# P times V in two PSUM banks of 256 queries, instead of one bank of 512, in a gated mix of segment attention and SwiGLU

## The chip, the cores and the metric

The kernel runs on one NeuronCore of a Trainium2 chip. The metric is the device time of one execution in microseconds (us), taken as the median of three timed executions; beside it there is one profiled execution, whose trace all readings come from. The engines are called by what they do here: TensorE multiplies matrices and writes its sums to PSUM, VectorE and ScalarE read PSUM and write SBUF, GpSimd works on SBUF alone, and SyncE issues transfers.

## The reference

The input x has 2048 rows of 640. The output is `g * a + (1 - g) * b`, with a gate `g = sigmoid(x . gate_w)` per row, an attention branch a and a SwiGLU branch b with an inner width of 1728. The attention has 32 heads of 20 columns and walks over 4 segments of 512 rows. The part that matters here, for each head and segment:

```
logits = einsum("bhqd,bhkd->bhqk", qs, ks) * scale + mask      # causal within the segment
p      = softmax(logits)
a_dot  = einsum("bhqk,bhkd->bhqd", p, vs)
o      = g * a_mem + (1 - g) * a_dot        # a_mem: read from a running memory M, z
M, z   = M + phi(ks)^T vs,  z + sum(phi(ks))
```

## The kernel before

TensorE's order is written out by hand: the program order of matmuls is the order in which the Python code issues them. The other engines' orders come from a scheduler. All projections (`q`, `k`, `v`, `g` and `u` of the SwiGLU, `f` its down projection, `op` the output projection) are long runs of 128x128x512 matmuls, and they fill the time between short attention bursts, called visits here.

A quad is four heads. Each quad of attention has a large visit and a small one. In its large visit TensorE issues, without a projection between them, `s_fill` 0 and `t_fill` 0 and 1, then `pv_quad` of a quad from an earlier visit, then `t_fill` 3, `s_fill` 2, `t_fill` 2 and `s_fill` 1 (the list `VISITS`, line 758). `s_fill` (line 594) makes logits with queries on the partitions, and VectorE takes row maxima of them (line 609). `t_fill` (line 625) makes logits with keys on the partitions, and ScalarE takes their exponent out of PSUM into the tile P (line 641). `pv_quad` (line 650) multiplies the exponents by V: the four heads stand in four column groups of 32 of the array and run side by side. Key block kb needs only queries from 128 kb on, so the four key blocks give widths of 512, 384, 256 and 128 queries. An fp32 matmul appears in the trace as two instructions, so one quad has 32 of them. Its sums are one tile `o` of 128 x 512, which VectorE copies to the SBUF tile `oq` (line 659); a transfer stores `oq` to DRAM (line 661).

PSUM has 8 banks, and every tile in it takes one whole bank. `bank_tile` (line 111) gives the banks out in a queue:

```
k = free.pop(0)
ps = pp.tile([P, L], F32, tag=f"b{k}", name=name, bufs=1)
if hold:
    held[k] = -hold
else:
    free.append(k)
```

A projection's bank is held out of the queue until its last matmul (`filled`, line 122). At a large visit none is held, so a tile takes the bank of the tile that was taken eight places before it, and its first matmul waits until the last reader of that older tile has ended. An `s_fill` and a `t_fill` take two banks each, a `pv_quad` one. The first eight tiles of a visit are two of `s`, four of `t`, the `o`, and the first `t` of `t_fill` 3.

The readers of the projections' tiles that stand just ahead of a visit also run on VectorE or ScalarE: line 515 multiplies a `g` tile by the tanh that ScalarE made of it, line 521 reads a `u` tile, line 285 and then line 287 read a `q` or `k` tile (phi), and lines 536, 561, 563 and 816 read `f` and `op` tiles.

Of the kernel before, what the change touches and what calls it, by code (L numbers as in the profile page):

```python
# [17 lines left out]
P = 128  # L18
# [16 lines left out]
PSEG = ((0, 512), (512, 384), (1024, 256), (896, 128))  # L35
# [3 lines left out]
def gated_mix(ctx: ExitStack, tc: tile.TileContext, xT, wqk, wv, w13, w2, w2h, wo, beta, out):  # L39
    nc = tc.nc  # L40
# [70 lines left out]
    def bank_tile(name, hold=None):  # L111
# [8 lines that stand above are left out]
        return ps  # L120
# [447 lines left out]
    oall, heads, pairs = {}, {}, {}  # L568
# [80 lines left out]

    def pv_quad(p):  # L650

        ps = bank_tile(f"o{p}")
        for kb, (o, n) in enumerate(PSEG):
            for i in range(4):
                nc.tensor.matmul(ps[32 * i:32 * i + 32, kb * P:], heads[2 * p + i]["v"][:, kb],  # L655
                                 pairs[p + i // 2]["P"][:, i % 2, o:o + n],
                                 start=kb == 0, stop=kb == 3, skip_group_check=True)
        ot = sp.tile([P, L], F32, tag="oq", name=f"oq{p}", bufs=1)
        nc.vector.tensor_copy(ot, ps)
        c, h = heads[2 * p]["c"], heads[2 * p]["h"]  # L660
        nc.sync.dma_start(od[c][h:h + 4].rearrange("h e n -> (h e) n"), ot)
        q = p // 2 % 8
        for b in OUT.get(q, ()):
            after(8, o_load, c, b)
        if q == 7:
            after(6 if c < NSEG - 1 else 2, o_sums, c)
# [77 lines left out]
    def after(n, f, *a):  # L744
        soon.append([n, f, a])
# [15 lines left out]
    def attention():  # L761

        for m in range(-1, NQUAD + 2):
            for n in range(40):
                if m == -1 and n < 40 - LEAD:
                    continue

                todo = VISITS.get(n, ()) if m != 1 else {BIG: VISITS[BIG][:3], BIG + 6: VISITS[BIG][4:]}.get(n, VISITS.get(n, ()))
                todo = [(kind, m - q, f) for kind, q, *f in todo if 0 <= m - q < NQUAD]
                if todo:  # L770
                    yield "amid" if len(todo) < 4 else "between"
                    for kind, q, f in todo:
                        if kind == "o":
                            pv_quad(2 * q)
                        else:
                            (s_fill if kind == "s" else t_fill)(q, *f)
                    if n == SMALL and 0 <= m < NQUAD:
                        after(4, max_rows, 2 * m)
                elif n in ((24, 36) if m < 0 else (BIG + 7, SMALL + 1)) and m + 1 < NQUAD:
                    load_pair(2 * (m + 1) + (n > BIG + 7 if m >= 0 else n > 24))  # L780
                tick()
                yield m
# [262 lines left out]
```

## Time and profile before

| | us |
|---|---|
| median of three timed executions | 1108.73 (1108.67 to 1112.61) |
| the profiled execution | 1108.07 |
| its span, first to last instruction | 1106.4 |
| TensorE matmuls busy | 1095.1 |
| VectorE busy | 593.5 |
| GpSimd busy | 583.3 |
| ScalarE busy | 381.2 |

The profiled execution is 0.66 us below the median, and 1.67 us of it lie outside the span. The granted clock of TensorE is 1.000 over the span. Busy times of TensorE are modelled from pipelined instructions; where it matters, the starts of its instructions are read instead, in the timeline. In the timeline's rows the first column is the start of an instruction or of a merged run, the second its duration, both in us, and square brackets hold the idle time of the engine ahead of it with what ended it. Buffer numbers are left out of tile names.

### The profile page before, as it was taken

How to read it: one execution, taken by the hardware profiler on the slowest of the kernel's cores; microseconds unless marked ns; L12 is line 12 of the kernel's file. 1: busy time of each engine (PE TensorE's matmuls, PEld its weight loads, DVE VectorE, ACT ScalarE, POOL GpSimd, SP SyncE). 2: the span in 40 equal slices, each digit the busy share in tenths (PEclk: the TensorE clock that was granted, in tenths of full speed). 3: DMA queues.
4: the chain of work that ended last, by engine and by line, in shares of the span. 5: the costliest groups of instructions: out<-in, count | busy, mean ns of one | idle time of the engine just before them, and what ended most of it. 6: DMA issues, size and time to landing. Idle time of an engine off the chain costs nothing.

```text
span 1106.4 us, 17867 instructions
## 1 busy us (share of the span) xinstructions
PE 1095.1 (99%) x6285; PEld 854.0 (77%) x6285; DVE 593.5 (54%) x1708; ACT 381.2 (34%) x826; POOL 583.3 (53%) x729
## 2 busy tenths in 40 slices
PE   9999999999999999999999999999999999999997
PEld 7988877777777777787977777777777777777786
DVE  5032564355555554366154678875557665551645
ACT  6244233343233122145244543424333332233120
POOL 5055556366366363565175547556764555565253
PEclk9999999999999999999999999999999999999999
DMA  8266943335165132535268967455654443432122
GB/s 314 102 212 220 281 117 82 95 82 127 47 164 125 57 78 94 156 98 191 96 202 271 287 204 193 103 157 138 166 139 111 103 104 90 117 105 86 52 79 95
DMA packets 87545, 153.20 MB, mean 138 GB/s; under 512 B 11584, under 2 KB 25184, under 8 KB 87456
## 3 DMA queue, kind: packets, MB, share of 16 engines
q1 hardware_dynamic: 63040, 106.30, 30.5%
q0 software_dynamic: 20384, 38.68, 15.6%
q10 hardware_dynamic: 4032, 7.08, 1.8%
q8 instruction: 50, 0.82, 0.3%
q14 instruction: 39, 0.32, 0.1%
HBM read 96.56 MB, written 54.54 MB: 137 GB/s over the span
## 4 chain that ended last, share of the span: by engine, by line
PE 94%; DVE 3%; ACT 1%; DMA 1%; issue 1%; ACTq 0%; SPq 0%; DVEq 0%
PE g L253 17%; PE u L253 16%; PE f L555 16%; PE k L253 6%; PE v L381 6%; PE op L805 6%; PE o L655 6%; PE q L253 5%; PE s L602 5%; PE t L635 4%; PE nd L348 1%; PE pm L445 1%; PE q L323 1%; DVE junk L609 1%; PE pkt L430 1%
## 5 line engine op out<-in xcount | busy, mean ns | idle before, releaser
L609 DVE CUSTOM_DVE_ANT_0 junk<-s,mask 128x256 bf16<-128x256 f32 (+3 forms) x512 | 250.3, 489 | 105.9 <-PE s L602 73.6
L641 ACT ACTIVATE P<-t 128x512 f32<-128x512 f32 (+1 forms) x384 | 172.4, 538 | 190.5 <-PE t L635 153.3
L253 PE MATMUL g<-X,W 128*128 128x512 f32 x840 | 208.7, 398 | 0.0
L175 POOL TENSOR_TENSOR W<-wr,W 128x640 fp32r<-128x640 f32 (+1 forms) x126 | 200.2, 1595 | 2.3
L174 POOL CAST W<-wr 128x640 fp32r<-128x640 f32 (+1 forms) x126 | 90.9, 726 | 208.9 <-PE f L555 47.0
L253 PE MATMUL u<-X,W 128*128 128x512 f32 x780 | 196.8, 399 | 0.0
L555 PE MATMUL f<-ht,W 128*128 128x512 f32 x820 | 196.6, 397 | 0.0
L645 POOL TENSOR_SCALAR_AFFINE_SELECT P<-P 128x256 f32<-128x256 f32 x192 | 94.0, 498 | 181.1 <-ACT P L641 180.7
L253 PEld LDWEIGHTS g<-X,W 128*128 128x128 f32 x840 | 156.0, 188 | 36.5 <-issue 0.4
L555 PEld LDWEIGHTS f<-ht,W 128*128 128x128 f32 x820 | 152.8, 188 | 36.5 <-DVE acc L536 0.4
L253 PEld LDWEIGHTS u<-X,W 128*128 128x128 f32 x780 | 144.1, 188 | 34.4 <-ACT P L641 0.3
L107 POOL TENSOR_TENSOR ht<-ft,ht 128x512 fp32r<-128x512 f32 x52 | 67.0, 1289 | 91.9 <-ACT ht L106 91.3
L579 POOL DMA_DIRECT2D qk<-qkd x128 | 83.3, 652 | 0.3
L602 PE MATMUL s<-qk 60*128 60x256 f32 (+3 forms) x512 | 78.2, 346 | 1.3 <-DVE fu L515 1.0
L253 PE MATMUL k<-X,W 128*128 128x512 f32 x300 | 77.0, 404 | 0.0
L655 PE MATMUL o<-P,vg 128*32 128x512 f32 (+3 forms) x1024 | 75.5, 436 | 1.4 <-DVE on L735 1.4
L514 ACT ACTIVATE ft<-g 128x512 f32<-128x512 f32 x52 | 31.1, 599 | 125.8 <-PE g L253 114.8
L381 PE MATMUL v<-W,X 128*128 128x320 f32 (+1 forms) x480 | 71.9, 311 | 0.4 <-ACT P L641 0.4
L515 DVE SCALAR_TENSOR_TENSOR fu<-ft,g 128x512 f32<-128x512 f32 x52 | 35.6, 685 | 68.3 <-ACT ft L514 59.2
L381 PEld LDWEIGHTS v<-W,X 128*128 128x128 f32 x480 | 71.0, 189 | 1.1 <-ACT P L641 0.6
L106 ACT CAST ht<-ft 128x512 fp32r<-128x512 f32 x52 | 32.2, 619 | 112.0 <-DVE ft L521 111.9
L563 DVE TENSOR_TENSOR acc<-f,acc 128x512 f32<-128x512 f32 x65 | 44.7, 689 | 44.8 <-PE f L555 44.6
(120 smaller groups left out, 1200.6 us busy)
## 6 DMA issues: line engine op xcount, KB each, us to landing
qk<-qkd POOLq DMA_DIRECT2D x128, 240.0 KB, 4.2
wr<-in_w_dram SPq DMA_DIRECT2D x80, 320.0 KB
qkd<-qs SPq DMA_DIRECT2D x20, 512.0 KB
qkd<-ks SPq DMA_DIRECT2D x20, 512.0 KB
od<-oq SPq DMA_DIRECT2D x32, 256.0 KB
wr<-in_wo_dram SPq DMA_DIRECT2D x20, 320.0 KB
vg<-vd SPq DMA_DIRECT2D x16, 336.0 KB
xr<-in_xT_dram SPq DMA_DIRECT2D x20, 256.0 KB
```

The lines of the kernel that those rows point to most:

```text
L107: (lo or nc.gpsimd.tensor_sub)(dst[:, 1], src, dst[:, 0].bitcast(F32))
L174: nc.gpsimd.tensor_copy(w[:, 0, :n], raw[:, :n])
L175: nc.gpsimd.tensor_sub(w[:, 1, :n], raw[:, :n], w[:, 0, :n].bitcast(F32))
L253: nc.tensor.matmul(ps, w[:, a, kb * P:(kb + 1) * P], x[:, b, kb, :], start=n == 0, stop=n == 14)
L381: nc.tensor.matmul(ps[:, :n1 - n0], x[:, a, kb, lb * P:(lb + 1) * P], wvt[kb][:, b, n0:n1], start=n == 0, stop=n == 14)
L555: nc.tensor.matmul(ps, w, h, start=n == 0, stop=n == len(ms) - 1)
L579: here(nc.gpsimd.dma_start(t[64 * i:64 * i + RH], qkd[c][RH * (h + i):RH * (h + i + 1)]))
L602: nc.tensor.matmul(ps[i][:, o:o + w], q[:, qb * P:(qb + 1) * P], key[:, :w], start=n == 0, stop=n == len(todo) - 1, skip_group_check=True)
L609: nc.vector.tensor_tensor_reduce(out=junk[:, :w], in0=ps[i][:, o:o + w], in1=mask[:, L - w:], scale=1.0, scalar=-3.0e38, op0=ALU.add, op1= ...
L641: last["exp"] = nc.scalar.activation(pairs[2 * m + k]["P"][:, i, o:o + n], ps[i][:, b:b + n], AF.Exp, scale=SCALE)
L645: nc.gpsimd.affine_select(d, d, pattern=[[0, 2], [0, n], [1, P]], base=0, channel_multiplier=-1, compare_op=ALU.is_ge, fill=0.0)
L655: nc.tensor.matmul(ps[32 * i:32 * i + 32, kb * P:], heads[2 * p + i]["v"][:, kb], pairs[p + i // 2]["P"][:, i % 2, o:o + n], start=kb == 0 ...
```

## The change

`pv_quad` takes two banks instead of one. The first holds queries 0 to 255 and gets key blocks 0 (256 wide) and 1 (128 wide). The second holds queries 256 to 511 and gets key blocks 0, 1 and 2 (256 wide each) and 3 (128 wide). The products are the same; the 16 matmuls of a quad become 24 (32 and 48 instructions). VectorE's copy of 512 columns becomes two of 256 columns; the first waits for the first bank only. The order of all other matmuls stays as it was, but every tile after the first half of `o` takes its bank one place further along the queue.

```diff
     def pv_quad(p):
 
-        ps = bank_tile(f"o{p}")
-        for kb, (o, n) in enumerate(PSEG):
-            for i in range(4):
-                nc.tensor.matmul(ps[32 * i:32 * i + 32, kb * P:], heads[2 * p + i]["v"][:, kb],
-                                 pairs[p + i // 2]["P"][:, i % 2, o:o + n],
-                                 start=kb == 0, stop=kb == 3, skip_group_check=True)
+        halves = [bank_tile(f"o{p}_{x}")[:, :256] for x in range(2)]
+        for x, ps in enumerate(halves):
+            todo = [(kb, max(P * kb, 256 * x), 256 * x + 256) for kb in range(2 * x + 2)]
+            for n, (kb, q0, q1) in enumerate(todo):
+                o = PSEG[kb][0] + q0 - P * kb
+                for i in range(4):
+                    nc.tensor.matmul(ps[32 * i:32 * i + 32, q0 - 256 * x:], heads[2 * p + i]["v"][:, kb],
+                                     pairs[p + i // 2]["P"][:, i % 2, o:o + q1 - q0],
+                                     start=n == 0, stop=n == len(todo) - 1, skip_group_check=True)
         ot = sp.tile([P, L], F32, tag="oq", name=f"oq{p}", bufs=1)
-        nc.vector.tensor_copy(ot, ps)
+        for x, ps in enumerate(halves):
+            nc.vector.tensor_copy(ot[:, 256 * x:256 * x + 256], ps)
         c, h = heads[2 * p]["c"], heads[2 * p]["h"]
         nc.sync.dma_start(od[c][h:h + 4].rearrange("h e n -> (h e) n"), ot)
```

## The prediction

> **What bounds the kernel now.** I read the page first: busy times, then the chain that ended last.
>
> ```profile
> span 1106.4 us, 17867 instructions
> PE 1095.1 (99%) x6285; PEld 854.0 (77%) x6285; DVE 593.5 (54%) x1708; ACT 381.2 (34%) x826; POOL 583.3 (53%) x729
> ...
> PE 94%; DVE 3%; ACT 1%; DMA 1%; issue 1%; ACTq 0%; SPq 0%; DVEq 0%
> ```
>
> TensorE (PE) carries 94% of the chain, and nothing else more than 3%. So the end moves by what TensorE's stream gains or loses; a faster VectorE (DVE) pays only where TensorE waits for it. I therefore looked at one large visit in the timeline, the first that has an `o`, starting at 172.24.
>
> ```profile
> 172.24 2.36 PE L655 MATMUL o<-P,vg 128*32 128x512 f32 x32
> 172.48 0.68 DVE L515 SCALAR_TENSOR_TENSOR fu<-ft,g 128x512 f32<-128x512 f32 x1
> 172.69 0.13 PEld L655 LDWEIGHTS o<-P,vg 128*32 128x32 f32 x4 [0.30 <-issue]
> 173.08 0.68 DVE L609 CUSTOM_DVE_ANT_0 junk<-s,mask 128x512 bf16<-128x512 f32 x1
> 173.12 0.13 PEld L655 LDWEIGHTS o<-P,vg 128*32 128x32 f32 x4 [0.30 <-issue]
> 173.44 0.13 PEld L655 LDWEIGHTS o<-P,vg 128*32 128x32 f32 x4 [0.19 <-issue]
> 173.77 0.56 PEld L655 LDWEIGHTS o<-P,vg 128*32 128x32 f32 x12 [0.19 <-issue]
> 174.53 0.50 PE L635 MATMUL t<-qk 62*128 62x512 f32 x2
> 174.66 0.69 DVE L659 COPY oq<-o 128x512 f32<-128x512 f32 x1 [0.89 <-PE o L655]
> 175.12 2.19 ACT L641 ACTIVATE P<-t 128x512 f32<-128x512 f32 x6 [0.96 <-PE t L635]
> 175.34 0.57 PE L602 MATMUL s<-qk 60*128 60x384 f32 x4
> 175.84 3.74 PE L253 MATMUL u<-X,W 128*128 128x512 f32 x15
> ```
>
> Two things are to be seen. First, the last `s_fill` of the visit waits for the copy: its second tile is the eighth after `o`, so it takes `o`'s bank, and the copy ends at 174.66 + 0.69 = 175.35, just after that fill began at 175.34. Second, the copy idles 0.89 us for TensorE before it can start. Where the copy is out of the way, the same fill is shorter:
>
> ```profile
> 557.78 2.36 PE L655 MATMUL o<-P,vg 128*32 128x512 f32 x32
> 559.65 0.69 DVE L287 SCALAR_TENSOR_TENSOR pk<-k,phi_t 128x512 f32<-128x512 f32 x1
> 560.40 0.50 PE L635 MATMUL t<-qk 62*128 62x512 f32 x2 [0.27 <-DVE pk L287]
> 561.22 0.40 PE L602 MATMUL s<-qk 60*128 60x384 f32 x4
> ```
>
> It takes 0.40 us here against 0.57: the wait is worth at most 0.17 us. This visit also shows the other kind of wait. The `t` tile after `o` takes the bank of the last projection tile ahead of the visit, a `k` here; line 287 ends with it at 559.65 + 0.69 = 560.34, and `t` starts 0.06 later, at 560.40. It is 2.62 us behind the start of `o`, against 2.29 (174.53 less 172.24) in the first visit. So 0.06 us is the price from a reader's end to TensorE's start.
>
> **Part 1: narrower matmuls.** A group is four instructions side by side, one per head; a quad has 8 groups before and 12 after, over the same columns. The weight loads start as each group begins: 172.69 to 173.12 is a 512-wide group, 0.43; 173.12 to 173.44 and 173.44 to 173.77 are 384-wide, 0.32 and 0.33. That is 0.108 per 128 columns in both, so nothing is left for a group as such; the rounding leaves at most 0.01. Four more groups in 32 quads are 128, so 0 to 1.3 us; a group cheaper than its columns is excluded by the same rows. I take 0.3, near the lower end, since 4 to 3 fits the two sorts of rows. The first group shows 0.45 (172.24 to 172.69), 0.02 over: the load of the first weights, which is exposed only after a pause.
>
> The Trainium skill speaks against such a split: "TensorEngine Tiling (Array Packing)", section Instruction Overhead, gives each matmul an overhead of about 60 cycles. By it, 16 more instructions in 32 quads at 25 ns (an estimate from that page and the 2.4 GHz of "TensorE: Matmul & The Clock Gate") would be 12.8 us, and the sum further down 18.5 instead of 6.0. The 0.43 and 0.32 above do not agree with it.
>
> **Part 2: the wait for the copy goes.** What the copies cost, by the nearest shapes:
>
> ```profile
> L609 DVE CUSTOM_DVE_ANT_0 junk<-s,mask 128x512 bf16<-128x512 f32 x128 | 88.2, 689 | 50.2 <-PE s L602 42.7
> L609 DVE CUSTOM_DVE_ANT_0 junk<-s,mask 128x256 bf16<-128x256 f32 x128 | 54.3, 424 | 38.1 <-PE s L602 30.9
> L641 ACT ACTIVATE P<-t 128x512 f32<-128x512 f32 x256 | 137.0, 600 | 190.5 <-PE t L635 153.3 <-DVE acc L563 18.7 <-DVE acc L816 9.0
> ```
>
> A row-maximum over 512 columns takes 689 ns, as the copy does (0.69), and one over 256 takes 424; so I give each half copy 0.42. The first starts when VectorE has done the maxima ahead of it, 173.08 + 0.68 = 173.76, and ends at 174.18. The second starts where the whole copy did, 174.66, and ends at 175.08, 0.27 earlier. After the change the last `s_fill` has the banks of the two halves, and both copies are over before 175.34. Its wait goes.
>
> What is late next is ScalarE. The projection that follows (175.84) takes the bank of the first `t` after `o`, whose exponent starts at 175.12 and lasts 0.60 by the group's mean: 175.72, plus 0.06 is 175.78. So 0.06 of the 0.17 is gained. Of the 32 visits with an `o` the last two have no such fill, and the three of part 3 that wait for line 287 or so start what follows behind ScalarE as well; 27 times 0.06 is 1.6. I take 1.5, since some fillers go straight on to the bank of the second `t` tile, which ScalarE frees later. Ends: 0, and 27 times 0.17 = 4.6 if ScalarE does not bind.
>
> **Part 3: a new wait at the second half.** The second half of `o` is now the eighth tile after the last projection tile ahead of the visit, a place that the `t` after `o` had before. That `t` came 2.29 us after `o`'s start; the second half is wanted after two groups of 256 and two of 128 columns, 6 times 0.108 = 0.65 us. The reader of that projection tile has 1.64 us less. Who is late is read visit by visit: the start of `o`, and the end of the reader.
>
> ```profile
> 342.09 2.36 PE L655 MATMUL o<-P,vg 128*32 128x512 f32 x32
> 341.29 0.69 DVE L521 SCALAR_TENSOR_TENSOR ft<-fu,u 128x512 f32<-128x512 f32 x1 [2.02 <-PE u L253]
> 976.35 2.36 PE L655 MATMUL o<-P,vg 128*32 128x512 f32 x32
> 976.60 0.68 DVE L515 SCALAR_TENSOR_TENSOR fu<-ft,g 128x512 f32<-128x512 f32 x1
> 512.43 2.36 PE L655 MATMUL o<-P,vg 128*32 128x512 f32 x32
> 513.68 0.68 DVE L287 SCALAR_TENSOR_TENSOR pq<-q,phi_t 128x512 f32<-128x512 f32 x1
> 629.55 2.36 PE L655 MATMUL o<-P,vg 128*32 128x512 f32 x32
> 631.36 0.69 DVE L287 SCALAR_TENSOR_TENSOR pq<-q,phi_t 128x512 f32<-128x512 f32 x1
> 632.11 0.50 PE L635 MATMUL t<-qk 62*128 62x512 f32 x2 [0.20 <-DVE pq L287]
> ```
>
> - A `u` tile (line 521) is read by 341.98, before `o` starts: no wait. Other kinds of tiles are no later than the 0.65.
> - A `g` tile is read by line 515 in the visit itself, since ScalarE's tanh comes between. It is the last projection in eight visits: the first at 172.24, read by 173.16, 0.92 behind; the last at 976.35, read by 977.28, 0.93 behind. TensorE stands from 0.65 to 0.92 + 0.06, and pays the 0.02 of the first weights: 0.33 to 0.35; with 0.33, 8 times is 2.6 us.
> - Three visits stand behind line 287. The `q` before 512.43 is read by 514.36, 1.93 behind: 1.93 + 0.06 - 0.65 = 1.34. The `k` before 557.78 is 2.56 behind: 1.97, less the 0.33 that `t` waited there already: 1.64. The `q` before 629.55 is read by 632.05, 2.50 behind: 1.91, less 632.11 - 629.55 - 2.29 = 0.27: 1.64. Together 4.6.
>
> Queued behind the waiting matmul is TensorE's whole order, and behind the second copy VectorE's maxima of `s_fill` 2 and 1; both move with it, so the visit and all after it start later by the wait. Nothing gives it back, because TensorE waits for almost nothing else. The lower end is 4.6 (only the three long waits), the upper 7.2. No row excludes that one is shortened, but each has both its ends in rows, so I take 7.2. A bank was short at one place before; the change asks for one more in the densest stretch.
>
> "Perfetto Trace Analysis" of the Trainium skill, section Matmuls, advises groups to rotate through PSUM banks so that a copy overlaps the next group. By it the change would bring the gain of part 2 alone, the time of the first rival below; the row of line 515, ending 0.92 us into `o`, is where this trace does not agree.
>
> The store of `oq` follows the second copy as it followed the whole one, and SyncE's queue ahead of it is unchanged here; ScalarE's order is unchanged too, GpSimd's and SyncE's only by neighbours that change places. None of these is on the chain with more than 1%, so they cost nothing unless a weight tile comes late.
>
> **Sum.** 7.2 + 0.3 - 1.5 = +6.0. On the profiled execution (1106.4 in the span, 1108.07 in all) that is 1114.1; the median stood 0.66 above it, so 1108.73 + 6.0 = 1114.7, or 0.54% slower. A difference under 0.5% (5.5 us, about what a measurement here can tell from no change) is hardly further away.
>
> **Rivals.**
>
> - Not slower. All readers of part 3 are done by 0.59 us into `o` (0.65 less 0.06), so no visit waits, and part 2's gain stands: 1108.73 + 0.3 - 1.5 = 1107.5. For it: most visits are so already, the `u` row among them. Against: VectorE is given line 515 behind the first maxima of the same visit, in an order that the change leaves alone. 0.07.
> - Only the long waits cost: VectorE reads the `g` tiles sooner, and 4.6 + 0.3 - 1.5 gives 1112.1. For: the `g` waits are short, and a little earlier tanh removes them. Against: 0.92 and 0.93 at both ends of the kernel. 0.08.
> - The second copy comes late: were VectorE busy over 0.48 us longer (174.66 less 174.18), the two copies take 0.84 instead of 0.69, and the last `s_fill` waits 0.15 longer in 27 visits: 1108.73 + 7.2 + 0.3 + 4.0 = 1120.2. For: line 287's visits, where VectorE has no idle time. Against: the 0.89 above. 0.09.
> - Each added group exposes its weight load:
>
> ```profile
> L655 PEld LDWEIGHTS o<-P,vg 128*32 128x32 f32 x1024 | 30.2, 110 | 42.8 <-issue 33.3 <-DVE ks L285 0.3
> ```
>
>   128 groups at 110 ns are 14.1 us, so 1114.4 + 14.1 = 1128.5 (6.0 without the 0.3). Against: the 0.43 to 0.32 of part 1. This is the form that the Trainium skill's rule of part 1 would take. 0.04.
>
> **How the numbers follow.** The forecast has 0.72. Its bounds: low 7.2 - 4.6 = +2.6, so 1111.3; high 7.2 + 1.3 = +8.5, so 1117.2. This range takes in the rival at 1112.1 and leaves out 0.07 + 0.09 + 0.04 = 0.20. Of the forecast's 0.72 I put 0.16 below 1114.3 (within 0.5%), because the sum is only 0.4 us beyond that line, and 0.56 above. Slower: 0.56 + 0.09 + 0.04 = 0.69. Same: 0.16 + 0.08 and the not-slower rival's 0.07, less 0.02 = 0.29. Faster: 0.02, that rival with the whole 4.6 gained.
>
> **What would show it.** In the profile after: the last `s_fill` of a visit takes 0.40 instead of 0.57; what follows it starts 3.54 instead of 3.60 behind `o` where nothing waited; gaps of about 0.33 within `o` in eight visits with line 515 as releaser, and of 1.3, 2.0 and 1.9 near 512, 558 and 630 with line 287; `t` after `o` no longer waits there. The half copies take about 420 ns. It is wrong if `o` has no gaps, if its 12 groups take more than 2.3 us without one, or if the time after a visit is made good later.

## The result, and the profile after

The change makes the kernel slower: the median of five executions is 1116.46 us (1115.28 to 1118.71), against 1110.20 (1108.67 to 1112.61) for five of the kernel before, a ratio of 1.0066 [1.0054, 1.0079]. On 1108.73 us that ratio is 7.3 us, where 6.0 was forecast. The profiled execution took 1115.73 us. These lines of its page answer to the first ones of before (span, busy times, chain of waits):

```profile
span 1114.0 us, 18957 instructions
PE 1094.7 (98%) x6797; PEld 863.1 (77%) x6797; DVE 599.9 (54%) x1740; ACT 381.2 (34%) x826; POOL 583.4 (52%) x729
...
PE 88%; DVE 6%; DMA 2%; issue 2%; ACT 1%; POOL 1%; ACTq 0%; SPq 0%; DVEq 0%; POOLq 0%
```

TensorE has no more work than before (1094.7 us against 1095.1); VectorE's share of the chain goes from 3% to 6%. So the time went into waits. The waits of TensorE and of its weight loads, summed by what ended them (us in total, times, longest), name them:

```profile
PE o L658 <- DVE pq L287: 3.4, 2, 1.9
PE o L658 <- DVE pk L287: 1.9, 1, 1.9
...
PE s L602 <- DMA qk<-qkd: 1.2, 1, 1.2
...
PEld o L658 <- DVE fu L515: 3.2, 8, 0.4
```

`o` now waits for line 287 in three visits and for line 515 in eight. The first large visit, in the timeline after:

```profile
172.48 2.70 PE L658 MATMUL o<-P,vg 128*32 128x256 f32 x48
172.72 0.68 DVE L515 SCALAR_TENSOR_TENSOR fu<-ft,g 128x512 f32<-128x512 f32 x1
173.46 1.45 PEld L658 LDWEIGHTS o<-P,vg 128*32 128x32 f32 x32 [0.39 <-DVE fu L515]
173.93 0.42 DVE L663 COPY oq<-o 128x256 f32<-128x256 f32 x1
175.11 0.50 PE L635 MATMUL t<-qk 62*128 62x512 f32 x2
175.25 0.42 DVE L663 COPY oq<-o 128x256 f32<-128x256 f32 x1 [0.90 <-PE o L658]
175.93 0.40 PE L602 MATMUL s<-qk 60*128 60x384 f32 x4
```

The second half's weights come at 173.46, just after line 515 ends at 172.72 + 0.68 = 173.40, and `t` starts 2.63 us behind `o` instead of 2.29. Both halves are copied before the last `s_fill`, which takes 0.40 us instead of 0.57. The saving is there, and smaller than the wait. What sets its size is in two more rows of this visit:

```profile
175.70 1.64 ACT L641 ACTIVATE P<-t 128x512 f32<-128x512 f32 x4 [1.30 <-PE t L635]
176.35 0.76 PEld L253 LDWEIGHTS u<-X,W 128*128 128x128 f32 x4 [0.23 <-ACT P L641]
```

ScalarE's first exponent behind `o` starts at 175.70; with the 0.60 us of one such instruction it ends at 176.30, and the weights of the next projection, which takes that bank, are loaded 0.05 later. A visit whose projection tile is read early has the saving alone:

```profile
342.90 2.37 PE L658 MATMUL o<-P,vg 128*32 128x256 f32 x48
345.20 0.50 PE L635 MATMUL t<-qk 62*128 62x512 f32 x2
...
346.44 0.73 PE L253 MATMUL g<-X,W 128*128 128x512 f32 x2
```

`t` stands 2.30 behind `o`, and the next projection 3.54, where before it stood 3.60 behind.

### The profile page after: what moved, and what is told of

The parts are those of the page before. It is cut to its first block, busy times and chain, and to the rows that moved or that the text cites. A ratio compares the mean times of both kernels' runs of the same rounds, so it can differ in the third digit from the quotient of the medians.

```text
span 1114.0 us, 18957 instructions
## 1 busy us (share of the span) xinstructions
PE 1094.7 (98%) x6797; PEld 863.1 (77%) x6797; DVE 599.9 (54%) x1740; ACT 381.2 (34%) x826; POOL 583.4 (52%) x729
## 4 chain that ended last, share of the span: by engine, by line
PE 88%; DVE 6%; DMA 2%; issue 2%; ACT 1%; POOL 1%; ACTq 0%; SPq 0%; DVEq 0%; POOLq 0%
PE f L555 16%; PE g L253 16%; PE u L253 15%; PE k L253 6%; PE v L381 6%; PE op L809 6%; PE o L658 6%; PE q L253 5%; PE s L602 4%; PE t L635 3%; DVE junk L609 2%; PE nd L348 1%; PE pm L445 1%; PE q L323 1%; DVE fu L515 1%
## 5 line engine op out<-in xcount | busy, mean ns | idle before, releaser
L658 PE MATMUL o<-P,vg 128*32 128x256 f32 (+1 forms) x1536 | 78.1, 346 | 7.7 <-DVE pq L287 3.4
L602 PE MATMUL s<-qk 60*128 60x256 f32 (+3 forms) x512 | 73.7, 340 | 2.5 <-DMA qk<-qkd 1.2
L658 PEld LDWEIGHTS o<-P,vg 128*32 128x32 f32 x1536 | 44.8, 109 | 37.1 <-DVE pq L287 3.9
```

What stands on the lines that cost most here:

```text
L602: nc.tensor.matmul(ps[i][:, o:o + w], q[:, qb * P:(qb + 1) * P], key[:, :w], start=n == 0, stop=n == len(todo) - 1, skip_group_check=True)
L658: nc.tensor.matmul(ps[32 * i:32 * i + 32, q0 - 256 * x:], heads[2 * p + i]["v"][:, kb], pairs[p + i // 2]["P"][:, i % 2, o:o + q1 - q0], s ...
```

## The experiments

The theory is the prediction's: the narrow groups are nearly free, the copy's end is on TensorE's path, and the loss comes from the bank of the second half, which a projection's reader still holds. The main rival is that more, narrower matmuls cost time themselves. Every ratio below is against the kernel before, measured beside it on the same chip; square brackets hold its 95% interval. For the kernels that are edited out of before, the diff is against before, for the others against the change.

**`narrow_one_bank`**: the 12 narrow groups, but in the two halves of one bank, and one copy of 512.

```diff
-        ps = bank_tile(f"o{p}")
+        whole = bank_tile(f"o{p}")
+        halves = [whole[:, 256 * x:256 * x + 256] for x in range(2)]
...
-        nc.vector.tensor_copy(ot, ps)
+        nc.vector.tensor_copy(ot, whole)
```

> The matmuls of the change (12 narrow groups a quad) go into the two halves of one bank, with one copy of 512 columns after them, so no bank is taken in addition. My theory: +0.3 us against the kernel before (10 ns a quad), the last s_fill of a visit still 0.57 us long, no gap within o. Rival (each added group costs a weight load or a fixed overhead of some 25 ns an instruction): +12.8 to +14 us, and the t after o starts about 2.7 us behind o instead of 2.30.

Measured: 1109.34 us against 1109.07, ratio 1.0002 [0.9993, 1.0011]. The timeline of its first visit:

```profile
172.70 2.37 PE L659 MATMUL o<-P,vg 128*32 128x256 f32 x48
...
175.00 0.50 PE L635 MATMUL t<-qk 62*128 62x512 f32 x2
...
175.81 0.57 PE L602 MATMUL s<-qk 60*128 60x384 f32 x4
```

`t` stands 2.30 behind `o` with 48 instructions, against 2.29 with 32, and the last `s_fill` is back at 0.57. The 512 added instructions cost no more than the 0.01 us a quad of these rows, some 0.3 us in all, which the times can't tell from nothing. So the waits and the saving both come with the second bank and the copy that it lets start early.

**`two_copies_one_bank`**: the matmuls and the bank of before, with two copies of 256 behind them.

```diff
-        nc.vector.tensor_copy(ot, ps)
+        for x in range(2):
+            nc.vector.tensor_copy(ot[:, 256 * x:256 * x + 256], ps[:, 256 * x:256 * x + 256])
```

> The kernel before, with its one bank and its wide matmuls, but two copies of 256 columns, both after the last matmul. My theory: the second copy ends 0.08 to 0.15 us later than the whole one did (2 times 0.42 less an overlap of some 0.08, against 0.69), the last s_fill waits for it and TensorE's stream moves by as much in some 27 visits: +2 to +4 us. Rival (the copy is hidden, so the gain of 0.06 a visit in the change is no gain of the copy): 0 us, the last s_fill stays 0.57 us long.

Measured: 1112.66 against 1109.07, ratio 1.0040 [1.0025, 1.0055], 4.4 us (2.8 to 6.1), where 2 to 4 were expected.

```profile
175.80 0.76 DVE L660 COPY oq<-o 128x256 f32<-128x256 f32 x2 [0.89 <-PE o L655]
...
176.47 0.70 PE L602 MATMUL s<-qk 60*128 60x384 f32 x4
```

The last `s_fill` takes 0.70 instead of 0.57, and 27 visits pay 0.13, which is 3.5. Two short copies together end later than one long one, but only by 0.07 (0.76 less 0.69); where the other 0.06 of a visit come from, no run settles. So the copy's end does stand on TensorE's path before, as part 2 says. The lateness of the second copy, a rival, is a real price too, but only without a second bank.

**`second_half_other_bank`**: the change, with the second half's bank taken one place later in the queue.

```diff
-        halves = [bank_tile(f"o{p}_{x}")[:, :256] for x in range(2)]
+        halves = [bank_tile(f"o{p}_0")[:, :256]]
+        free.insert(1, free.pop(0))
+        halves.append(bank_tile(f"o{p}_1")[:, :256])
```

The projection's bank then goes to the `t` behind `o`, as before the change. Copies, groups and store are those of the change.

> The change, but the second half of o takes the bank of the first s tile of its visit, and the t after o takes the bank of the last projection tile, as it did before the change. My theory (the loss is the wait for the projection tile's reader): the gaps of 0.33 and 1.3 to 2.0 us in o go, the t waits of 0.33 and 0.27 of the kernel before come back, the gain at the last s_fill stays; -1.2 us against the kernel before, 8 us below the change. Rival (the loss comes with the matmuls, the copies or the transfers that happen to land later): stays at +6 to +7 us.

Measured: 1108.18 against 1109.07, ratio 0.9992 [0.9983, 1.0000]. The rows that waited in the change, in this kernel:

```profile
172.36 2.37 PE L660 MATMUL o<-P,vg 128*32 128x256 f32 x48
174.66 0.50 PE L635 MATMUL t<-qk 62*128 62x512 f32 x2
...
559.18 0.50 PE L635 MATMUL t<-qk 62*128 62x512 f32 x2 [0.39 <-DVE pk L287]
...
630.96 0.51 PE L635 MATMUL t<-qk 62*128 62x512 f32 x2 [0.17 <-DVE pq L287]
```

The waits at the second half are gone, and what is left at `t` is about what before had (0.27 and 0.20). The ratio gives -0.9 us, where -1.2 was forecast. Its interval reaches 1, so that the kernel is below before is barely shown; that it is far below the change, which is 7.3 above before, is clear. The second half now takes the bank of the visit's first `s` tile, which costs one new wait: in the visit near 678 it waits 0.35 us for a row maximum, and `t` stands 2.59 behind `o`. One line that picks another bank takes the whole loss away. That settles the mechanism.

**`other_bank_three_visits`**: the same exchange only in the three visits with line 287.

```diff
-        halves = [bank_tile(f"o{p}_{x}")[:, :256] for x in range(2)]
+        halves = [bank_tile(f"o{p}_0")[:, :256]]
+        if p in (22, 24, 28):
+            free.insert(1, free.pop(0))
+        halves.append(bank_tile(f"o{p}_1")[:, :256])
```

> The same exchange of banks only in the three visits with line 287 (o near 512, 558 and 630 us); all others as in the change. My theory: 4.6 of the 7.2 us of waits go, eight waits of 0.33 us stay: about +1.4 us against the kernel before. Rival (only the long waits cost, the eight short ones are made good later in the kernel): -1.2 us, level with the kernel that exchanges the banks everywhere.

Measured: 1110.61 against 1109.07, ratio 1.0014 [1.0006, 1.0023], 1.5 us, where 1.4 was forecast. Against the exchange in all visits (-0.9) the eight waits for line 515 cost 2.4, with 2.6 forecast; they are paid, and the second rival (only the long waits cost) falls.

**`before_again`** and **`change_again`**: the two kernels as they are, for a second trace of each.

> The kernel before, profiled once more. If the 0.6 us around 505 us and the 0.7 to 1.3 us around 949 us, by which every later trace differs from the first one, belong to that one execution, this trace has them too and its span is 0.1 to 0.6 us longer than 1106.4; if they belong to the kernels compared, it repeats the first trace.

> The change once more, beside the kernels of this set: 0.6 to 0.7% over the kernel before; o with the same gaps to 0.02 us; the wait for a qk transfer near 949 us of another length than 1.2 us if it varies by execution, of the same length if the change makes it.

Measured: 1111.1 for the one execution of before (span 1109.4); 1116.13 (1114.79 to 1119.45) for the change against 1109.94, ratio 1.0060 [1.0046, 1.0073]. The waits in the change's visits repeat. The span of this second trace of before is 3.0 us longer than that of the first, though at most 0.6 was expected. The difference near 505 us is one of executions: from the visit that starts near 467 to the next it takes 44.64 us in the first trace of before, 43.77 in the second and 44.72 in that of `before_load_from_sync`, against 43.78 in the first of the change. A thing that moves is one transfer, the load of `qk` near 949 us (before) or 956 (changed). Its rows in the first trace of before, in the second of before, and in the first of the change:

```profile
948.76 1.06 PE L602 MATMUL s<-qk 60*128 60x512 f32 x2
949.48 0.80 PE L635 MATMUL t<-qk 62*128 62x512 f32 x6
```

```profile
948.70 0.50 PE L602 MATMUL s<-qk 60*128 60x512 f32 x1
950.74 0.47 PE L602 MATMUL s<-qk 60*128 60x512 f32 x1 [1.55 <-DMA qk<-qkd]
950.87 1.20 PE L635 MATMUL t<-qk 62*128 62x512 f32 x6
952.00 3.57 PE L655 MATMUL o<-P,vg 128*32 128x512 f32 x32
955.50 0.50 PE L635 MATMUL t<-qk 62*128 62x512 f32 x2
```

```profile
955.01 0.50 PE L602 MATMUL s<-qk 60*128 60x512 f32 x1
956.71 0.46 PE L602 MATMUL s<-qk 60*128 60x512 f32 x1 [1.21 <-DMA qk<-qkd]
956.87 0.78 PE L635 MATMUL t<-qk 62*128 62x512 f32 x6
```

From the `s` to the `t` it takes 0.72, 2.17 and 1.86 us; the visit at 341.99 in the trace of the change took 0.34 (342.33 less 341.99). So both kernels wait there, before 0.4 us in one execution and 1.8 in another.

The second trace of before shows what such a wait can cost beyond itself. Behind it `o` takes 3.57 us instead of 2.36, and `t` stands 3.50 behind it instead of 2.29: the granted clock of TensorE is 0.50 over 951.4 to 954.4 us, and 1.00 over 948 to 951 and over 955 to 958. Two more traces below have such a stretch of half clock, each behind a wait of TensorE: `change_load_from_sync` (0.50 over 636.3 to 639.3, behind a wait of 1.68 us) and `far_bank` (0.50 over 950.8 to 953.8, behind 1.42). The first trace of the change has waits of 1.46 and 1.90 us and no such stretch, so what decides stays open.

**`change_load_from_sync`**, **`before_load_from_sync`**: this one load goes into SyncE's queue, in the change and in before.

```diff
-            here(nc.gpsimd.dma_start(t[64 * i:64 * i + RH], qkd[c][RH * (h + i):RH * (h + i + 1)]))
+            dst, src = t[64 * i:64 * i + RH], qkd[c][RH * (h + i):RH * (h + i + 1)]
+            here(nc.sync.dma_start(dst.bitcast(F32), src) if p == 60 else nc.gpsimd.dma_start(dst, src))
```

> The change, with the two qk loads that the visit near 949 us waits for issued from SyncE's queue instead of GpSimd's, where they stand behind two weight tiles. My theory (the landing of these loads ends that visit's first wait): the wait goes, about 1.1 us less than the change. Rival (transfers are hidden as the prediction had it): no difference.

> The kernel before, with only the two qk loads ahead of the visit near 949 us issued from SyncE. My theory: that visit's transfer wait goes in this kernel as well, 1 to 1.5 us less; the copy's wait at the last s_fill stays. Rival (the wait is the change's): 0.

Measured: the change with it, 1114.96 against 1109.94, ratio 1.0050 [1.0037, 1.0062]; before with it, 1107.74 against 1108.62, ratio 0.9992 [0.9983, 1.0000]. The wait in the waits of TensorE, first of the change with the moved load, then of before with it:

```profile
PE s L603 <- DMA qk<-qkd: 0.3, 1, 0.3
```

```profile
PE s L603 <- DMA qk<-qkd: 0.2, 1, 0.2
```

The wait goes in both kernels, so it is not a cost of the change. By the times it is worth about 1 us in each (1.1 and 0.9), which neither interval tells from nothing. With the load moved in both, the change stands at 1.0050 / 0.9992 = 1.0058 of before (from two separate measurements, so no interval is given). The profiled execution of the change with the load moved is 1116.44 us, 1.5 above its median; the visit near 633 has the half clock:

```profile
636.05 3.11 PE L659 MATMUL o<-P,vg 128*32 128x256 f32 x32 [1.68 <-DVE pq L287]
```

Its second half takes 3.11 us, where 1.72 is usual behind such a wait.

**`far_bank`** and **`far_bank_and_sync_load`**: the projection's bank is put back five places in the queue instead of one. The second half takes the next bank as in `second_half_other_bank`, and the projection's bank goes to the first `t` of `t_fill` 2, which is wanted later than the `t` behind `o`; in the second kernel the load is moved as well.

```diff
-        halves = [bank_tile(f"o{p}_{x}")[:, :256] for x in range(2)]
+        halves = [bank_tile(f"o{p}_0")[:, :256]]
+        free.insert(5, free.pop(0))
+        halves.append(bank_tile(f"o{p}_1")[:, :256])
```

> The last projection tile's bank put five places back in the queue, without moving the two qk loads. My theory: only the t waits of 0.33 and 0.27 of the exchange go, 0.6 us; so -1.5 us against the kernel before, and the transfer wait near 949 us is there (0.8 to 1.5 us). Rival (all of the 2.2 us between the exchange and the kernel with both edits comes from the banks): -3 us or more.

> The change with the last projection tile's bank put five places back in the queue, so that the second half of o, both t tiles and the first s tile after it take banks of the visit's own first tiles, and the t of t_fill 2 takes the late bank; with the two loads from SyncE as well. My theory: no gap in o, no wait of 0.33 and 0.27 at t near 560 and 632 us, no transfer wait near 949: some 0.6 and 1.1 us below the exchange of two banks, so 1.5 to 3 us below the kernel before (0.1 to 0.3%). Rival (the waits move to the tiles that now take the late banks): level with the exchange of two banks, 0.1% below the kernel before.

Measured: `far_bank` 1107.88 against 1108.62, ratio 0.9995 [0.9986, 1.0004]; `far_bank_and_sync_load` 1105.94 against 1109.94, ratio 0.9966 [0.9953, 0.9979], the fastest kernel of the study, faster than both kernels (its interval lies below 1, and the change's above). That is 3.8 us, more than the 1.5 to 3 forecast and more than the 0.6 and 0.9 us of its two edits taken singly; the rest is not explained, and how often half clock follows the load's wait in executions without a trace is not known. The visit that waited for line 287 both before and after the change, in `far_bank`:

```profile
557.25 2.37 PE L660 MATMUL o<-P,vg 128*32 128x256 f32 x48
559.55 0.50 PE L635 MATMUL t<-qk 62*128 62x512 f32 x2
```

`t` is 2.30 behind `o`, without a wait. By its rows `far_bank` gains what was left at `t` (0.39 and 0.17 above); by its time it is not told apart from before, nor from the exchange by one place. In its profiled execution TensorE waits 1.4 us for the load of `qk` near 949, and in the half clock behind that `t` stands 3.82 behind `o` instead of 2.30.

**`far_bank_two_swaps`**: on top of that, another bank for the first half at two quads, because one visit near 700 still waits 1.33 us at `o`.

```diff
+        if p in (26, 34):
+            free.insert(1, free.pop(0))
         halves = [bank_tile(f"o{p}_0")[:, :256]]
```

> The far bank with both loads from SyncE, and in two visits (o near 601 and 701 us) the first half takes the bank of the last projection tile and the late bank of the one before it goes five places back. My theory: the wait of 1.3 us at the start of o near 701, for line 735's reader, goes: 1.3 us less than the same kernel without it, 4 to 5 us below the kernel before. Rival (o waits there for something else, such as the masked P): level with the kernel without it.

Measured: 1106.30 against 1108.62, ratio 0.9980 [0.9969, 0.9991], no gain over the kernel without the swaps, where 1.3 us was forecast. The visit without and with them:

```profile
698.20 0.50 PE L603 MATMUL s<-qk 60*128 60x512 f32 x2
700.51 2.37 PE L661 MATMUL o<-P,vg 128*32 128x256 f32 x48 [1.33 <-DVE on L742]
702.81 0.50 PE L636 MATMUL t<-qk 62*128 62x512 f32 x2
```

```profile
698.81 0.50 PE L603 MATMUL s<-qk 60*128 60x512 f32 x2
699.92 2.37 PE L663 MATMUL o<-P,vg 128*32 128x256 f32 x48
702.52 0.68 DVE L610 CUSTOM_DVE_ANT_0 junk<-s,mask 128x512 bf16<-128x512 f32 x1
703.26 0.50 PE L636 MATMUL t<-qk 62*128 62x512 f32 x2 [0.97 <-DVE m L610]
```

The wait at `o` goes and one at `t` takes its place: from the first `s` to that `t` it takes 4.45 instead of 4.61. VectorE itself is late there (that row maximum ends at 703.20), so a bank helps by 0.16 only.

## Why the prediction was right, and where it was not

- Part 1, right. Narrow groups were put at 0.3 us, and `narrow_one_bank` measures 1.0002 [0.9993, 1.0011]. The overhead of about 60 cycles that the Trainium skill gives a matmul ("TensorEngine Tiling (Array Packing)", section Instruction Overhead) would be 12.8 us by the estimate above; as a cost added to each matmul that does not fit the ratio, nor 2.30 us for 48 instructions beside 2.29 for 32. The same section says that a matmul with a free dimension of 1 takes as long as one of 60; read so, as a floor under short matmuls, it is not against these rows, whose narrowest matmul has 128 columns. The exposed weight loads, 14.1 us as a rival, fall with the ratio too.
- Part 2, right. The last `s_fill` takes 0.40, where nothing waited the next instruction mostly stands 3.54 or 3.55 behind `o` instead of 3.60, with ScalarE next as forecast, and a half copy takes what the row maximum of 256 columns suggested:

```profile
L663 DVE COPY oq<-o 128x256 f32<-128x256 f32 x64 | 27.0, 422 | 30.5 <-PE o L658 30.5
```

- Part 3, the eight waits: right, 0.33 to 0.34 each in the rows.
- Part 3, the three long waits: right in place and cause, too small in size. The term was 1.34 + 1.64 + 1.64 = 4.6. `t` behind `o` came at 3.97, 4.41 and 4.41 us, where before it came at 2.29, 2.62 and 2.56: 1.68, 1.79 and 1.85, together 5.3. The step that failed is the end of line 287: part 3 took it from before (1.93, 2.56 and 2.50 us behind `o`), as if the change left VectorE's order alone. That order is claimed only for line 515, and there it held. The visits near 512, 558 and 630 after the change:

```profile
512.68 0.86 PE L658 MATMUL o<-P,vg 128*32 128x256 f32 x16
513.93 0.41 DVE L663 COPY oq<-o 128x256 f32<-128x256 f32 x1
514.27 0.67 DVE L287 SCALAR_TENSOR_TENSOR pq<-q,phi_t 128x512 f32<-128x512 f32 x1
515.00 1.72 PE L658 MATMUL o<-P,vg 128*32 128x256 f32 x32 [1.46 <-DVE pq L287]
516.65 0.50 PE L635 MATMUL t<-qk 62*128 62x512 f32 x2
...
561.38 0.41 DVE L663 COPY oq<-o 128x256 f32<-128x256 f32 x1
561.71 0.68 DVE L287 SCALAR_TENSOR_TENSOR pk<-k,phi_t 128x512 f32<-128x512 f32 x1
...
634.87 0.41 DVE L663 COPY oq<-o 128x256 f32<-128x256 f32 x1
635.20 0.68 DVE L287 SCALAR_TENSOR_TENSOR pq<-q,phi_t 128x512 f32<-128x512 f32 x1
```

  Before, line 287 stood ahead of the copy (631.36 the product, 631.98 the copy; 513.68 and 514.85). Now the first half's copy, which the change lets start early, stands between line 285 and line 287 in all three visits and starts some 0.34 us ahead of the very reader that the second half waits for (513.93 and 514.27, 561.38 and 561.71, 634.87 and 635.20). Line 287 ends 2.26, 2.70 and 2.71 us behind the start of `o` (near 512: 514.27 + 0.67 less 512.68) instead of 1.93, 2.56 and 2.50. It is 0.33, 0.14 and 0.21 us later, together the 0.7 us that the term lacked. `second_half_other_bank`, which has the early copy without the wait at the second half, shows the same near 558: the copy stands ahead, line 287 ends 2.70 behind `o`, and `t` stands at 2.76, where `narrow_one_bank`, without an early copy, has 2.62. No run moved the copy behind line 287 alone.
- Transfers, put at nothing "unless a weight tile comes late". A `qk` load came late, in both kernels. It does not explain the ratio, since moving it leaves 1.0058, but it stands in the spans of the two first profiles: of 1114.0 - 1106.4 = 7.6 us, 1.1 are this load (1.86 less 0.72), while some 0.8 near 505 went the other way.
- The sum: with the visits as measured, the eight waits come to 2.7 and the three to 5.3, and 27 times 0.05 is saved: 2.7 + 5.3 - 1.3 = 6.7 us, where 6.0 was forecast. Read directly, the stretches from `o` to the first instruction behind the visit, summed over all 32 visits, are 6.5 us longer in the first trace of the change than in that of before. The same sum gives -1.0 for `second_half_other_bank` and 1.5 for `other_bank_three_visits`, whose times gave -0.9 and 1.5. The two ratios of the change give 7.3 (6.0 to 8.8) and 6.7 (5.1 to 8.1). 1116.46 lies 1.8 us above the 1114.7 forecast; 0.7 are the long waits. For the rest the runs show no step to blame: medians of the unchanged kernel ran from 1108.62 to 1110.20, and the forecast started from 1108.73. Whether some of the executions without a trace had stretches of half clock behind the new waits is not known.
- The not-slower rival is wrong of the change as made, but right of `second_half_other_bank`: "all readers are done" can be arranged by choosing the bank. There the advice to rotate through PSUM banks (the Trainium skill, "Perfetto Trace Analysis", section Matmuls) holds, with 0.9992 [0.9983, 1.0000] beside 1.0066 [1.0054, 1.0079] for the same two banks handed out in plain turn.

## What to carry to other kernels

When banks are given out in turn, a tile more shortens the way back for every tile behind it: for each tile, compare when it is wanted with when the last reader of its new bank ends, and put the tile that is wanted soonest into the bank that was read longest ago. A copy that can start earlier may also be scheduled ahead of an instruction that the critical engine waits for, so ask what it is now ahead of, not only when it ends. Taking one wait away is worth only the distance to the next one: 0.17 us was in sight at the copy, and 0.05 was gained before ScalarE came next. And where one trace of each kernel is compared, read the granted clock behind each long wait: in one execution of before the half clock behind a wait of 1.55 us cost 1.2 us beyond the wait.

## What the runs showed of the hardware that was not expected

- Column-tiled fp32 matmuls cost by their columns down to 128: 2.30 us for 48 instructions and 2.29 for 32 over the same columns.
- Two copies of 256 columns hold up TensorE 0.13 us longer than one of 512 (an `s_fill` of 0.70 instead of 0.57), though a copy alone takes 422 ns against 690. Two in a row take 0.76 together, not 0.84, as an instruction on VectorE can start before the one ahead of it has ended in the trace (513.93 + 0.41 is 514.34, and line 287 starts at 514.27).
- The same load, at the same place in GpSimd's order, makes TensorE wait 0.4 to 1.8 us from one execution to the next. From SyncE's queue the wait was 0.2 or 0.3.
- In three of the thirteen traces, a wait of TensorE of 1.42, 1.55 or 1.68 us was followed by some 3 us at a granted clock of 0.50, which cost another 1.2 to 1.5 us. Waits of 1.46 and 1.90 us in another trace were not.
